# Softmax weights of a masked attention copied by transfers into a rounded-format tile and transposed from it two iterations later

## The chip, the cores and the metric

One core of one Trainium2 chip runs the whole program. The time is device microseconds from the profiler's clock; the kernel before is timed in three runs, and one further execution is profiled. TensorE is called PE, its weight loads PEld, VectorE DVE, ScalarE ACT, GpSimd POOL, and SyncE, which here only queues transfers, SP.

## What is computed

Attention over 4 batches of 8 heads, 576 tokens and 64 columns a head, in which scores that lie more than `tau` below their row's maximum are left out; then a mixture of 8 experts of which each token takes one; then a dense layer with a sigmoid-gated nonlinearity. The change touches the attention.

```python
def _attn_ref(q, k, v, tau):
    scale = 1.0 / np.sqrt(q.shape[-1])
    scores = scale * np.matmul(q, k.transpose(0, 1, 3, 2))
    thresh = np.max(scores, axis=-1, keepdims=True) - tau
    scores = np.where(scores >= thresh, scores, -1000000000.0)
    scores = scores - np.max(scores, axis=-1, keepdims=True)
    attn = np.exp(scores)
    attn = attn / (np.sum(attn, axis=-1, keepdims=True) + 1e-09)
    return np.matmul(attn, v)

def _moe_ref(x, modality_id, w_gate, modality_bias, w1, w2):
    logits = x @ w_gate + modality_bias[modality_id]
    e_idx = np.argmax(logits, axis=1)
    ...
    for e in range(E):
        mask = e_idx == e
        out[mask] = gate_w[mask, None] * (np.maximum(x[mask] @ w1[e], 0.0) @ w2[e])

def _moe2_ref(x, w_in, w_out):
    h = x @ w_in
    return (h * (1.0 / (1.0 + np.exp(-1.702 * h)))) @ w_out
```

## The kernel before

**Units.** Two heads make a pair; there are 16 pairs, and nine units to a pair (`UPP`), 144 in all. Units 0 to 7 are 128 queries of one head against its 576 keys; unit 8 holds the last 64 queries of both heads. A loop in `run` takes two units an iteration, 72 iterations, and one more to empty it. The order in which each engine works is the order in which the code issues.

**One iteration.** `qk` makes the scores of two units in PSUM (tile `sc`, L227), with queries and keys each split into a rounded part and a rest (`qkh`, `qkl`, type fp32r), so three products. `max` (DVE, L255) writes the shifted scores `e` and their extreme `thr`; `exp` (ACT, L261) exponentiates; `mask` (DVE, L285) drops what is below the threshold and writes the weights `E` (or `ET` for unit 8) and their row sum. The next unit on the same PSUM banks has to wait for that mask. `trans` (L313) transposes the weights of the two units of the iteration before, four 128x128 blocks a unit, in f32, into a PSUM tile `tr`, of which there are three; ACT copies it to `AT` (L315, L317). In four of nine iterations `trans_tails` (L331, L332, L335) transposes the last key columns, copied to `ATt` (L340). The table `AV` says how many value steps an iteration takes: four steps of products with V (L357), then a closing step (L363) and the copy to `xT` (L364), for each half of a pair. `ROW` says how many row items: products of `xT` with an identity and the gate's weights (L397), copied to `xr` (L402), scaled on POOL (L405, L410), and stored to `x_dram` by SP (L416).

**Loads.** SP queues a pair's queries and keys as one transfer of 896 KB (`F`, three buffers, L124) and its values (`V`, four buffers, L128) when a pair two or three earlier starts. POOL splits them, one piece an iteration: keys (L149 to L151), then queries of both heads. `sides` hands out small steps of the router (the choice of experts) between. `AVL`, `ROWL` and `SD` are the tables for the last batch's iterations, and `FILL` the number of dummy transposes that keep PE busy in the first ones. Behind the loop come the experts (L1033, L1077) and the dense layer (L1033, L1058), matmuls of fp32r parts with up to 512 columns.

## Time and profile before

| | us |
|---|---|
| median of 3 runs | 922.79 |
| lowest, highest | 922.45, 923.26 |
| the profiled execution | 921.75 |
| its span, first to last instruction | 920.0 |
| attention: first scores, last transposes | 5.7, 293 |

All durations below come from that one profiled execution. A busy time is the union of an engine's instructions, and matmuls overlap: an instruction's duration is longer than its distance to the next, so the length of a row of several shows more than the mean of one. The chain of waits goes back from the last instruction, at each step to what released it, and names the engine that held the end at that time. The table of windows gives each engine's busy time in a stretch, and at its end the granted clock, the mean share of the 16 DMA engines and their GB/s.

### The profile page before, as it was taken

What the parts mean: (1) busy time and instruction counts of PE and PEld (TensorE: products, weight loads), DVE (VectorE), ACT (ScalarE), POOL (GpSimd) and SP (SyncE); (2) the same over time, 40 slices, a digit from 0 to 9 for tenths busy, and PEclk for the clock granted to TensorE, in tenths of its full rate; (3) what the DMA queues carried; (4) which work ended last, traced back from release to release, by engine and by line L of the source; (5) the groups of instructions that cost most, each with busy time, mean ns of one, the idle gap of its engine ahead of it and who ended that gap; (6) DMA issues with size and microseconds to landing.
All of it is one profiled execution on the core that took longest, in us unless ns stands there. A gap on an engine that the chain in (4) does not pass through costs nothing.

```text
span 920.0 us, 14322 instructions
## 1 busy us (share of the span) xinstructions
PE 898.1 (98%) x5341; PEld 716.4 (78%) x5341; DVE 510.3 (55%) x1104; ACT 445.2 (48%) x787; POOL 233.2 (25%) x333
## 2 busy tenths in 40 slices
PE   9999999999999999999999999999999999999994
PEld 7677776776766788878889888888888888888894
DVE  7888889889787574678787588611111121111110
ACT  6777777777776533555545455422222222222221
POOL 7845655556544501010610000010001000100100
PEclk9999999999999999999999999999999999999997
DMA  7213432242102735465756153310001000100100
GB/s 257 73 46 122 140 128 72 71 131 74 36 9 76 239 103 187 142 230 178 229 183 231 68 184 117 112 46 12 24 12 46 7 12 7 46 0 1 46 1 26
DMA packets 53756, 85.67 MB, mean 93 GB/s; under 512 B 9300, under 2 KB 35058, under 8 KB 53682
## 3 DMA queue, kind: packets, MB, share of 16 engines
q1 hardware_dynamic: 50098, 74.63, 25.0%
q0 software_dynamic: 3312, 9.94, 3.3%
q8 instruction: 44, 0.72, 0.3%
q14 instruction: 30, 0.25, 0.1%
q10 hardware_dynamic: 272, 0.13, 0.0%
HBM read 67.57 MB, written 17.11 MB: 92 GB/s over the span
## 4 chain that ended last, share of the span: by engine, by line
PE 81%; DVE 7%; issue 6%; ACT 2%; DMA 2%; POOL 1%; SPq 0%; POOLq 0%; ACTq 0%
PE tr L1033 29%; PE sc L1058 19%; PE sc L1077 9%; PE sc L227 7%; PE av L357 6%; PE tr L313 6%; DVE E L285 3%; PE tr L397 2%; PE av L363 2%; DVE e L255 2%; ACT e L261 1%; DMA cv_raw<-in_moe_w_in_dram 1%; DMA xg<-y_first 1%; DVE bl L1303 1%; PE av L1005 1%
## 5 line engine op out<-in xcount | busy, mean ns | idle before, releaser
L1270 DVE TENSOR_TENSOR hl<-sg,hh 128x512 fp32r<-128x512 f32 (+1 forms) x80 | 51.1, 638 | 261.5 <-ACT hh L1268 259.1
L1267 ACT ACTIVATE sg<-tr 128x512 f32<-128x512 f32 (+1 forms) x80 | 44.3, 554 | 226.9 <-PE tr L1033 226.9
L261 ACT ACTIVATE e<-e,thr 128x576 f32<-128x576 f32 x144 | 109.6, 776 | 75.2 <-DVE e L255 74.6
L255 DVE TENSOR_SCALAR_CACHE_REDUCE e<-sc,taue 128x576 f32<-128x576 f32 x144 | 112.8, 815 | 33.7 <-PE sc L227 33.3
L1058 PE MATMUL sc<-wo_h,hh 128*128 128x512 f32 x288 | 112.2, 390 | 0.0
L1058 PE MATMUL sc<-wo_l,hh 128*128 128x512 f32 x288 | 112.2, 390 | 0.0
L1058 PE MATMUL sc<-wo_h,hl 128*128 128x512 f32 x288 | 112.0, 389 | 0.0
L285 DVE SCALAR_TENSOR_TENSOR E<-sc,thr,e 128x576 f32<-128x576 f32 x128 | 100.4, 813 | 5.1 <-ACT e L261 4.4
L1033 PE MATMUL tr<-xl,wi_h 128*128 128x512 f32 (+1 forms) x320 | 78.7, 368 | 0.0
L1033 PE MATMUL tr<-xh,wi_l 128*128 128x512 f32 (+1 forms) x320 | 78.7, 368 | 0.0
L1033 PE MATMUL tr<-xh,wi_h 128*128 128x512 f32 (+1 forms) x320 | 78.6, 368 | 0.0
L357 PE MATMUL av<-AT,V 128*64 128x288 f32 x512 | 77.3, 420 | 1.1 <-DVE ixs L933 0.6
L313 PE MATMUL tr<-ident,E 128*128 128x128 f32 x512 | 71.2, 279 | 0.0
L315 ACT COPY AT<-tr 128x512 f32<-128x512 f32 x128 | 68.2, 577 | 0.0
L1033 PEld LDWEIGHTS tr<-xh,wi_h 128*128 128x128 f32 x320 | 57.7, 188 | 11.1
L1033 PEld LDWEIGHTS tr<-xh,wi_l 128*128 128x128 f32 x320 | 56.9, 189 | 10.0
L1033 PEld LDWEIGHTS tr<-xl,wi_h 128*128 128x128 f32 x320 | 56.9, 189 | 9.9
L151 POOL TENSOR_TENSOR qkl<-F,qkh 128x640 fp32r<-128x640 f32 (+1 forms) x30 | 63.1, 2102 | 2.5
L313 PEld LDWEIGHTS tr<-ident,E 128*128 128x128 f32 x512 | 55.1, 141 | 10.3 <-issue 8.7
L1058 PEld LDWEIGHTS sc<-wo_h,hl 128*128 128x128 f32 x288 | 54.1, 188 | 11.3
L227 PE MATMUL sc<-qkh 64*128 64x288 f32 x320 | 57.0, 353 | 6.0 <-DVE E L285 4.2
L1058 PEld LDWEIGHTS sc<-wo_h,hh 128*128 128x128 f32 x288 | 54.1, 188 | 10.7
(262 smaller groups left out, 1578.2 us busy)
## 6 DMA issues: line engine op xcount, KB each, us to landing
F<-in_kq_dram SPq DMA_DIRECT2D x15, 896.0 KB
ra<-in_moe_w_dram SPq DMA_DIRECT2D x20, 512.0 KB
rb<-in_moe_w_dram SPq DMA_DIRECT2D x20, 512.0 KB
cv_raw<-in_moe_w_in_dram SPq DMA_DIRECT2D x16, 512.0 KB
cv_raw<-in_moe_w_out_dram SPq DMA_DIRECT2D x16, 512.0 KB
V<-in_vp_dram SPq DMA_DIRECT2D x16, 320.0 KB
x_dram<-xrow SPq DMA_DIRECT2D x72, 64.0 KB
y_rest<-blank SPq DMA_DIRECT2D x8, 256.0 KB
```

The costliest lines, as they stand in the source:

```text
L151: nc.gpsimd.tensor_sub(lo, x, hi.bitcast(F32))
L227: m = nc.tensor.matmul(self.banks[:, bank, 0:288], a[rs, q:q + 128], b[rs, k:k + 288], start=(n == 0), stop=(n == len(ops) - 1),).ins
L255: self.read(u, nc.vector.tensor_scalar(e, d["sc", w], self.taue[:, 0:1], 3.0e38, op0=ALU.add, op1=ALU.min, accum_out=thr))
L261: self.nc.scalar.activation(d["e", w], d["e", w], ACTF.Exp, bias=d["thr", w][:, 0:1], scale=-1.0)
L285: self.read(u, nc.vector.scalar_tensor_tensor(out=E.rearrange("p (a c) -> p a c", a=2), in0=d["sc", w], scalar=d["thr", w][:, 0:1], in1=d[ ...
L313: nc.tensor.transpose(tp[:, kc * 128:(kc + 1) * 128], E[:, k0 + kc * 128:k0 + (kc + 1) * 128], self.ident)
L315: return lambda: nc.scalar.copy(AT[:, h, :, c * 128:(c + 1) * 128], tp.rearrange("p (k c) -> p k c", k=4))
L357: nc.tensor.matmul(d["av"][h * 64:(h + 1) * 64, 0:288], d["V"][:, h, kc, :], d["AT"][:, h, kc, cols], start=(kc == 0), stop=False, skip_gr ...
L1033: nc.tensor.matmul(hps[:, 0:T], w[:, kd, :], blk[x][:, kd, 0:T], start=(i == 0), stop=(i == 11))
L1058: nc.tensor.matmul(y, h[:, cs], w, start=(f == 0 and i == 0), stop=(f == blk["nf"] - 1 and i == 2))
L1077: nc.tensor.matmul(blk["y"][d], w[:, ds], h[:, 0:T], start=(f == 0 and i == 0), stop=(f == last and i == 2))
L1270: return [upper, lambda: nc.vector.tensor_sub(hl, sg, hh.bitcast(F32))]
```

## The change

The weights are no longer transposed from `E`. Each unit's first 512 weights (for the second head of a pair, the last 512) go, behind its mask, by an SP transfer of 256 KB into a tile `R` of type fp32r (`lay`); the transfer copies the bits as they are. There are six such tiles. The transposes read `R` and an identity of the same type, two iterations after the scores instead of one, and stand at the end of the iteration, behind values and rows, with their copies at the end of ACT's. Tails are transposed as before. The tables of values and rows are new, and the last batch's have one iteration more. `F` has two buffers instead of three; a pair's load is two halves, each issued from POOL's list of pieces after the split that frees the buffer, and the queries are split one head at a time. Row stores are kept in a list and issued behind the next masks. The router's one sum of phase A uses a `tr` tile, the first iterations' dummy transposes are 60 instead of 54.

```diff
--- before.py
+++ after.py
@@ -25,12 +25,12 @@
 UPP = 9
 PJ = 9
 QW, KW = 1280, 640
-AV = (2, 2, 3, 3, 2, 2, 3, 2, 1)
+AV = (1, 3, 2, 3, 2, 2, 3, 2, 2)
 TURNS = ((0, 1), (2, 3))
 TAILS = {2: -1, 5: -2, 7: -2, 0: -1}
 IT_LAST = (NPAIR - HP) * UPP // 2
-AVL = (2, 2, 3, 2, 3, 2, 3, 2, 1, 2, 2, 3, 3, 2, 2, 3, 3, 2, 5)
-ROWL = (0, 1, 0, 1, 1, 1, 1, 1, 1, 0, 0, 0, 0, 1, 0, 1, 0, 1, 0)
+AVL = (1, 3, 2, 3, 2, 2, 3, 2, 2, 1, 3, 2, 3, 2, 2, 3, 2, 2, 1, 5)
+ROWL = (2, 0, 1, 0, 0, 1, 1, 1, 1, 1, 0, 0, 0, 0, 0, 0, 1, 0, 1, 1)
 NS0 = 7
 CA = (0, 1, 2, 2, 2, 2, 2, 2, 2, 2, 2, 2, 2, 2, 2, 2)
 CB = (0, 0, 0, 1, 0, 1, 0, 1, 0, 1, 0, 1, 0, 0, 0, 0)
@@ -40,12 +40,12 @@
 NBW = 6
 F0 = (0, 1, 0)
 NROW = 2
-FILL = (14, 12, 12, 12, 4)
+FILL = (14, 16, 12, 12, 6)
 SN = 1
 SD = (1, 2, 2, 2, 1)
 TAU_MAX = 104.0
 W_TOP = (1.875 - 2.0 ** -23) * 2.0 ** -96
-ROW = (0, 1, 0, 1, 1, 0, 1, 0, 1)
+ROW = (2, 0, 1, 0, 0, 0, 0, 1, 1)
 
 class Attention:
 
@@ -74,7 +74,8 @@
         self.banks = P("a_sc", 1, space=PSUM).tile([128, 4, 512], F32, name="sc")
         Q = lambda name, bufs: late_ctx.enter_context(tc.tile_pool(name=name, bufs=bufs, side="right"))
         cst = P("a_const", 1)
-        self.fp = P("a_f", 3)
+        self.fp = P("a_f", 2)
+        self.er = P("a_er", 6)
         self.ep = P("a_e", 4)
         self.ex = P("a_exp", 3)
         self.et = P("a_et", 2)
@@ -89,6 +90,8 @@
         self.rp = Q("a_rows", 2)
         self.rw = Q("a_xrow", 6)
 
+        self.idr = cst.tile([128, 128], F32R, name="idr")
+        nc.gpsimd.tensor_copy(self.idr, ident)
         self.cq = cst.tile([128, 1], F32, name="cq")
         self.taue = cst.tile([128, 1], F32, name="taue")
         self.tau = tau
@@ -118,10 +121,13 @@
                 )
 
 
-    def load(self, p):
-        d = self.st[p] = {}
-        d["F"] = F = self.fp.tile([128, KW + 2 * S], F32, name="F")
-        self.nc.sync.dma_start(F, self.kq[p])
+    def load(self, p, parts=(0, 1)):
+        if 0 in parts:
+            self.st[p] = {"F": self.fp.tile([128, KW + 2 * S], F32, name="F")}
+        n = (KW + 2 * S) // 2
+        for i in parts:
+            cs = slice(i * n, (i + 1) * n)
+            self.nc.sync.dma_start(self.st[p]["F"][:, cs], self.kq[p][:, cs])
 
     def load_v(self, p):
         V = self.vp.tile([128, 640], F32, name="V")
@@ -142,7 +148,9 @@
     def split(self, p, i):
 
         nc = self.nc
-        x, (hi, lo) = (self.keys, self.queries)[i](p)
+        x, (hi, lo) = self.queries(p) if i else self.keys(p)
+        if i:
+            x, hi, lo = (t[:, i - 1] for t in (x, hi, lo))
         if i == 0 and p == 1:
             nc.scalar.activation(x, x, ACTF.Copy, scale=self.cq[:, 0:1])
         elif i == 0:
@@ -296,6 +304,16 @@
             ]
 
 
+    def lay(self, u):
+
+        p, w = divmod(u, UPP)
+        d = self.st[p]
+        c, h = divmod(w, 2)
+        E = d["E", 4] if w == 8 else d["E", c][:, h]
+        k0 = 64 if w < 8 and h == 1 else 0
+        d["R", w] = self.er.tile([128, 512], F32R, name="R")
+        self.nc.sync.dma_start(d["R", w].bitcast(F32), E[:, k0:k0 + 512])
+
     def trans(self, u):
 
         nc = self.nc
@@ -304,13 +322,12 @@
         c, h = divmod(w, 2)
         if w == 0:
             d["AT"] = self.at.tile([128, 2, 4, S], F32, name="AT")
-            d["ATt"] = self.at.tile([128, S], F32, name="ATt")
-        AT, ATt = d["AT"], d["ATt"]
+        AT = d["AT"]
         tp = self.ps_tr.tile([128, 512], F32, name="tr")
-        E = d["E", 4] if w == 8 else d["E", c][:, h]
-        k0 = 64 if w < 8 and h == 1 else 0
+        R = d.pop(("R", w))
         for kc in range(4):
-            nc.tensor.transpose(tp[:, kc * 128:(kc + 1) * 128], E[:, k0 + kc * 128:k0 + (kc + 1) * 128], self.ident)
+            cs = slice(kc * 128, (kc + 1) * 128)
+            nc.tensor.transpose(tp[:, cs].bitcast(F32R), R[:, cs], self.idr)
         if w < 8:
             return lambda: nc.scalar.copy(
                 AT[:, h, :, c * 128:(c + 1) * 128], tp.rearrange("p (k c) -> p k c", k=4))
@@ -323,6 +340,8 @@
         nc = self.nc
         p, w = divmod(u, UPP)
         d = self.st[p]
+        if w == 3:
+            d["ATt"] = self.at.tile([128, S], F32, name="ATt")
         ATt = d["ATt"]
         c0 = 0 if w == 3 else 2
         n = 256
@@ -413,7 +432,8 @@
                 rr.unsqueeze(3).broadcast_to([w, 2, 2, 64]),
             )
             for u in range(2 if kc < 4 else 1):
-                nc.sync.dma_start(xd[b, 2 * kc + u][:, hh * 256:(hh + 1) * 256], xrow[u * 64:(u + 1) * 64, :])
+                self.stores.append(lambda u=u: nc.sync.dma_start(
+                    xd[b, 2 * kc + u][:, hh * 256:(hh + 1) * 256], xrow[u * 64:(u + 1) * 64, :]))
             if hh == 1 and kc == 4:
                 items, gate = self.router.gate_items(b, lgt)
                 self.side.extend([None] * (1 if b == B - 2 else NROW) + items + self.router.after_batch(b, gate))
@@ -428,27 +448,29 @@
         rest = self.first()
         self.load_v(0)
         self.load_v(1)
-        self.load(2)
-        self.poolq = []
+        self.poolq, self.stores = [], []
         self.avq, self.rowq, self.side = avq, rowq, side = [], [], []
         side += [None] * NS0 + [self.gate_setup, *self.router.setup_items(self.setup), *self.extra]
         it = done = 0
         while done < NU:
             last = it >= IT_LAST
             us = [u for u in (2 * it, 2 * it + 1) if u < NU]
-            ts = [u for u in (2 * it - 2, 2 * it - 1) if 0 <= u < NU]
+            ts = [u for u in (2 * it - 4, 2 * it - 3) if 0 <= u < NU]
             starts = [u // UPP for u in us if u % UPP == 0]
             for p in starts:
-                if p + 3 < NPAIR:
-                    self.load(p + 3)
-                if p + 2 < NPAIR:
+                if 0 < p < NPAIR - 2:
                     self.load_v(p + 2)
                 for n in range(1 if p == 0 else p + 2, min(p + 3, NPAIR)):
                     self.poolq += [lambda n=n, i=i: self.split(n, i) for i in range(2)]
+                    if n + 2 < NPAIR:
+                        self.poolq += [lambda n=n: (self.split(n, 2), self.load(n + 2, (0,)))]
+                        self.poolq += [lambda n=n: self.load(n + 2, (1,))]
+                    else:
+                        self.poolq += [lambda n=n: self.split(n, 2)]
             k = it % 9
             for u in us:
                 self.qk(u)
-            copies = [self.trans(u) for u in ts]
+            copies = []
             if it > 1 and k in TAILS:
                 copies.append(self.trans_tails(2 * it + TAILS[k]))
             for i in range(2):
@@ -461,12 +483,17 @@
                 c()
             while rest:
                 rest.pop(0)()
+            if it == 0:
+                self.load(2)
+                self.load_v(2)
             if self.norm:
                 self.norm.pop(0)()
             for i, u in enumerate(us):
                 self.mask(u)
+                self.lay(u)
                 if last:
                     self.sides(SD[i + 2], False)
+            self.store()
             if it < len(FILL) and FILL[it]:
                 warm = self.ps_av.tile([128, 512], F32, name="av")
                 for _ in range(FILL[it]):
@@ -477,6 +504,8 @@
             while m and rowq:
                 rowq.pop(0)()
                 m -= 1
+            for c in [self.trans(u) for u in ts]:
+                c()
             n = 1 if it else 2
             while n and self.poolq:
                 self.poolq.pop(0)()
@@ -489,12 +518,18 @@
                     avq += self.av_items(p, w // 8)
             it += 1
 
+    def store(self):
+
+        while self.stores:
+            self.stores.pop(0)()
+
     def tail(self, n):
 
         for _ in range(n):
             for q in (self.avq, self.rowq):
                 if q:
                     q.pop(0)()
+                    self.store()
                     break
         return bool(self.avq or self.rowq)
 
@@ -918,7 +953,7 @@
 
         def sum_up(c0, c1):
             if c0 == 0:
-                t["ip"] = self.ps_av.tile([128, 512], F32, name="av") if first else self.ps_tr.tile([128, 512], F32, name="tr")
+                t["ip"] = self.ps_tr.tile([128, 512], F32, name="tr")
             for c in range(c0, c1):
                 nc.tensor.matmul(
                     t["ip"][:, 0:2 * nh], OL[:, c, :], R[:, c].rearrange("p i h -> p (i h)"),
```

PE, the third iteration of nine. Before, between its scores and the next, with `L313` the main transposes, `L335` the tails, `L357` and `L363` value steps:

```order
L227 MATMUL sc<-qkh_139,qkl_140 128x288 x2
L313 MATMUL tr<-ident,E 128x128 x8
L335 MATMUL tr<-ident,E 128x128 x2
L357 MATMUL av<-AT,V 64x288 x4
L363 MATMUL av<-ATt,V 128x288
L227 MATMUL sc<-qkh_139 128x288 x2
```

Now, with `L330` the main transposes, `L354` the tails, `L376` and `L382` value steps:

```order
L235 MATMUL sc<-qkh_144,qkl_145 128x288 x2
L354 MATMUL tr<-ident,E 128x128 x2
L376 MATMUL av<-AT,V 64x288 x2
L382 MATMUL av<-ATt,V 128x288
L330 MATMUL tr<-idr,R 128x128 x8
L235 MATMUL sc<-qkh_144 128x288 x2
```

The eight transposes moved from ahead of the values to just ahead of the next scores, and read `R`; this iteration takes one value step fewer.

SP in the loop, before (`L416` row stores, `L1164` the router's blank rows):

```order
L1164 DMA y_rest<-blank 128x512
L124 DMA F<-in_kq_dram 128x1792
L128 DMA V<-in_vp_dram 128x640
L1164 DMA y_rest<-blank 128x512
L416 DMA x_dram<-xrow 64x256 x2
L1164 DMA y_rest<-blank 128x512 x2
```

Now (`L315` the copies to `R`, `L130` halves of `F`, `L134` values, `L435` row stores, `L1199` blank rows):

```order
L315 DMA R<-E 128x512 x2
L435 DMA x_dram<-xrow 64x256
L130 DMA F<-in_kq_dram 128x896
L1199 DMA y_rest<-blank 128x512
L134 DMA V<-in_vp_dram 128x640
L315 DMA R<-ET 128x512
L315 DMA R<-E 128x512
L130 DMA F<-in_kq_dram 128x896
```

Two copies an iteration now stand in the same queue as the loads and stores, and behind them.

ACT in the first iteration of nine, before:

```order
L261 ACTIVATE e<-e,thr 128x576 x2
L315 COPY AT<-tr 128x4x128
L317 COPY AT<-tr 128x4x2x64
L340 COPY ATt<-tr 128x320
L364 COPY xT<-av 128x288
```

Now, with the exponentials at `L269`, tails `L359`, `xT` at `L383`, rows `L421`, transposed weights `L332`:

```order
L269 ACTIVATE e<-e,thr 128x576 x2
L359 COPY ATt<-tr 128x320
L383 COPY xT<-av 128x288
L421 COPY xr<-tr 128x288 x2
L332 COPY AT<-tr 128x4x128 x2
```

The copies of transposed weights moved behind all others, and two row copies came into this iteration.

## Rows read from the trace of the kernel before

**Rows 1.** The page: busy time of PE, and its slices and clock.

```profile
PE 898.1 (98%) x5341; PEld 716.4 (78%) x5341; DVE 510.3 (55%) x1104; ACT 445.2 (48%) x787; POOL 233.2 (25%) x333
...
PE   9999999999999999999999999999999999999994
...
PEclk9999999999999999999999999999999999999997
```

**Rows 2.** Windows: us busy, PE, PEld, DVE, ACT, POOL; clock, DMA share, GB/s.

```profile
100.00:150.00 50.00, 48.49 (x406) 34.34 (x404) 42.67 (x110) 36.48 (x69) 27.27 (x30) 1.00 0.27 85
```

**Rows 3.** Chain of waits: start us, us, engine, tile and line; PE alone.

```profile
113.19 0.98 PE sc L227 x10
114.18 1.03 PE tr L313 x8
...
117.01 1.00 PE sc L227 x11
```

**Rows 4.** Chain of waits where it goes round the loop.

```profile
129.37 0.61 PE sc L227 x6
...
130.00 0.04 DVE e L255
...
130.92 0.79 ACT e L261
...
131.73 1.56 DVE E L285 x4
```

**Rows 5.** Waits of 20 to 280 us: who for whom, total, times, longest.

```profile
DVE e L255 <- PE sc L227: 31.9, 53, 1.2
PEld sc L227 <- DVE E L285: 17.5, 39, 1.6
...
PE sc L227 <- DVE E L285: 3.4, 6, 1.1
```

**Rows 6.** Line L313: ns min/median/max, first and last start.

```profile
L313 PEld LDWEIGHTS tr<-ident,E x512: 137/140/144, 10.8 to 292.7; 128*128 128x128 f32 x171
L313 PE MATMUL tr<-ident,E x512: 272/273/332, 10.8 to 292.8; 128*128 128x128 f32 x171
```

**Rows 7.** Groups by line and shape: count, busy us, mean ns, idle before.

```profile
L332 PEld LDWEIGHTS tr<-ident,ET 128*64 128x64 f32 x16 | 1.8, 111 | 0.0
L357 PEld LDWEIGHTS av<-AT,V 128*64 128x64 f32 x512 | 30.7, 136 | 24.4 <-issue 11.1 <-ACT xT L364 0.9 <-PE av L923 0.6
L1033 PEld LDWEIGHTS tr<-xh,ah 128*128 128x128 f32 x160 | 27.2, 188 | 5.0 <-ACT xh L1006 0.8 <-DVE xl L1007 0.2
L1033 PE MATMUL tr<-xh,al 128*128 128x512 f32 x128 | 34.4, 390 | 0.0
L1033 PE MATMUL tr<-xh,al 128*128 128x264 f32 x32 | 5.1, 282 | 0.0
L402 ACT COPY xr<-tr 128x288 f32<-128x288 f32 x32 | 13.0, 409 | 1.1 <-PE tr L397 0.2
```

**Rows 8.** Timeline: start us, length, instruction; the first load and its use.

```profile
0.74 0.42 ACTq L162 DMA_DIRECT2D F<-in_kq_dram  x1
...
2.94 0.40 ACT L192 CAST qkh<-F 128x256 fp32r<-128x256 f32 x1 [0.25 <-DMA F<-in_kq_dram]
```

**Rows 9.** Timeline: the loop's end, and runs of four rounded matmuls.

```profile
291.55 0.82 DVE L285 SCALAR_TENSOR_TENSOR ET<-sc,thr,e 128x576 f32<-128x576 f32 x1
...
292.88 0.60 PE L313 MATMUL tr<-ident,ET 128*128 128x128 f32 x4
...
485.22 0.64 PE L1033 MATMUL tr<-xh,ah 128*128 128x264 f32 x4
...
601.60 1.07 PE L1033 MATMUL tr<-xh,wi_h 128*128 128x512 f32 x4
```

**Rows 10.** The page, DMA queues: packets, MB, share of 16 engines.

```profile
q1 hardware_dynamic: 50098, 74.63, 25.0%
```

**Rows 11.** Waits of SP's queue, 20 to 290 us.

```profile
SPq L692 <- POOL lgt L388: 22.5, 1, 22.5
```

## The prediction

> **What bounds the kernel now.** The page comes first: TensorE (PE) is busy 98% of the span and its granted clock stands at 0.9 or more of full speed in all slices but the last [rows 1]. That says which engine to look at, not what it waits for. The change touches the attention loop alone, so the next view is busy time by stages of 50 us: in the loop PE is busy almost throughout, VectorE (DVE) 42.67 of 50 us, ScalarE (ACT) 36.48, GpSimd (POOL) 27.27, and the DMA engines 0.27 of the time [rows 2]. Two units make an iteration; the transposes run from 10.8 to 292.8 us, 71.5 iterations, so one takes 3.94 us [rows 6].
>
> The chain of waits shows who holds an iteration. Most are PE alone: scores 0.98, transposes 1.03, then values and rows, 3.82 us from 113.19 to 117.01, with no other engine in the chain [rows 3]. Others are the loop: scores at 129.37, maximum, exponential, and the second mask ends at 133.29 [rows 4]. This loop starts its first maximum at 130.00, so DVE can't start another sooner than 3.29 us later. The waits agree: in 260 us PE waits 17.5 + 3.4 us for masks, and DVE 31.9 us for scores [rows 5]. With 66 iterations in there PE waits 0.32 us in each, so its own work is about 3.62 us. DVE's is 42.67/50 of 3.94, 3.36 us. So PE binds, with DVE and the loop 0.3 us below it: that is how much room a faster PE has before another stream binds.
>
> **The transposes.** The change leaves the number of main transposes: 144 units of four, 576. What they cost now: one lasts 273 ns, but four in a row last 0.60 us, so they follow each other at (0.60 - 0.27)/3 = 0.109 us [rows 6, 9]. No transpose of the rounded type, and no matmul of it below 256 columns, is in this trace, so the new price is bounded from neighbours. Rounded matmuls of 512 and 264 columns last 390 and 282 ns, 0.4355 ns a column; at 128 columns that makes 282 - 136 x 0.4355 = 223 ns, 50 less than now [rows 6, 7]. Their spacing at 512 columns is (1.07 - 0.39)/3 = 0.227 us [rows 9], which less 384 x 0.4355 ns is 0.060 us. That is the value I take: 0.049 saved each, **28.2 us** in 576. The lower end is 0.4355 x 128 = 0.056 us, 30.5 us saved.
>
> The upper end hangs on the weight load before each transpose. For a matmul 128 columns of weights take 188 ns and 64 take 136: 0.8 ns a column, some 104 ns of real work behind a fixed 84. For a transpose 128 take 140 and 64 take 111: 0.45 ns a column, 58 ns of work [rows 6, 7]. I take the second slope, since the type doesn't seem to set it: f32 weights of a matmul (136 for 64 columns) and rounded ones (188 for 128) lie on one line, and only the transposes lie below. If a rounded transpose loses this, its spacing is 0.104 or more and nothing is won.
>
> The Trainium skill (TensorE: Matmul & The Clock Gate, section LDWEIGHTS) gives one price for all, columns divided by 1.2, 107 ns for 128, with no case for a transpose. By that the present 0.109 would be the weight load's, and the 576 transposes would save 1 us. The trace agrees for matmuls (0.8 ns a column), and disagrees for transposes (0.45).
>
> **The copies.** Each unit's weights E now go by a transfer of 256 KB from SBUF to SBUF into R, queued on SyncE (SP) behind the mask; the transpose follows two iterations later. The hardware queue moved 74.63 MB in 25.0% of 16 engines' 920 us, a rate of 324 GB/s while busy, so a copy needs 0.81 us of all engines and two 1.62 an iteration; with today's 0.27 x 3.94 = 1.06 that is 2.7 of some 3.6 us [rows 2, 10]. They fit. Latency: the first 128 KB of queries are issued at 0.74 and used at 2.94, 2.2 us [rows 8]; twice the size makes it 2.6; behind a 448 KB half of a load 4.0, behind V also 5.0. The cover: the second mask ends 3.92 us after its iteration starts [rows 4], and the transposes that need its copy close the iteration two later, so before the next scores there are 3 periods. At 3.55 us that leaves 10.65 - 3.92 - 0.6 = 6.1 us. So I cost landing at nothing; the cover ends at 6.1 us.
>
> SP works in order, and what waits there now holds the copies too. F halves wait for the last split of their pair's buffer, V loads for the values that free theirs, stores of rows and gates for POOL; a gate's store waited 22.5 us once [rows 11], with nothing urgent behind it. The change moves the row stores behind the next masks, where POOL is done, and the order has the freeing value step in the iteration of the V load, ahead of its masks. POOL's query split in two pieces costs one more pair of instructions a pair of heads on an engine that is 55% busy [rows 2]; it is hidden, unless POOL is late for an F half.
>
> **What the new order gives back.** ACT copies the transposed weights after everything else of its iteration, and PSUM has three "tr" tiles. In the iteration with two row items (once in nine), tails, two rows and two transposes ask for five tiles. The second transpose needs the first row's copy, which stands behind both exponentials (the second ends near 129.37 + 3.1), the tail copy, the xT copy and its own, about 0.41 each [rows 4, 7]: 3.1 + 1.25 = 4.35 us after the start. PE comes there after scores of 0.98 [rows 3] and, an estimate, 2.5 us of tails, values, rows and a transpose, at 3.45. That is 0.9 us lost, eight times: 7.2. In the others PE's work is near 3.2 us against DVE's 3.36, and I add 0.8. Together **8 us** back; ends: 0 if those waits fall into time PE now waits anyway, 14 if the loop takes half.
>
> **Start and end.** F has two buffers instead of three, so the third pair's load comes after the first scores; it is needed nine iterations later. Six more warm-up transposes, 0.65 us, lie in the first iterations, before the values start: nothing. At the end, before, the last mask starts at 291.55 and its transposes run at 292.88 [rows 9]. Now 2.6 us of landing and one more, nearly empty, iteration (tail, one value item, one row, two transposes, some 1.5 to 2 us) stand between: **1.5 us** lost, from 0.5 to 3.
>
> **The sum.** The profiled execution took 921.75 us, 1.75 around its span of 920.0. 921.75 - 28.2 + 8 + 1.5 = 903.05; the median of the runs lies 1.04 above it: **904 us**. PE's slices behind the loop all read 9 up to the last [rows 1], so what is won before 293 us arrives at the end whole.
>
> **Rivals.** (1) DVE and the loop take over: PE has 3.23 us of work, DVE 3.36, and an in-order pair so evenly loaded loses more than I take. At 14 us back: 910. For it: the even load; against: DVE waits 31.9 us for scores now, and these come earlier. (2) The rounded transpose is no faster, held by its weight load: at a matmul's 0.104 it saves 3 us, at 0.119 (the spacing of a 264-column rounded matmul, from its four in 0.64 us [rows 7, 9]) it loses 6; with half of the order's 8 and the end's 1.5 the time is 925 to 934. For it: no such transpose is in the trace; against: the two slopes. The rule of the Trainium skill (TensorE: Matmul & The Clock Gate, section LDWEIGHTS) would end here. If the type needed more passes it would be later still; no row bounds that. (3) On the other side, landing: three periods hold mask, landing and transposes, so a period is (3.92 + landing + 0.7)/3 at least. It equals today's 3.94 at 7.2 us of landing; each us beyond costs 72/3 = 24. At 8 us the time is 943. For it: SP's waits of many us ahead of copies [rows 11]; against: 2.6 to 5 us by the sizes. The place to see it is PE's wait for R.
>
> **How the numbers follow.** Forecast 904: 0.58. Loop takes over, 910 to 918: 0.18. No faster transposes: 0.14, of which a little still ends faster through the evened-out value tables. Late landing: 0.10, mostly slower. A measurement tells 0.2%, 1.8 us, from no change, so faster (under 921) 0.78, same 0.08, slower 0.14. The range takes in the forecast's bounds (30.5 saved, nothing back, 0.5 at the end: 893) and the first rival, to 921; the rest, 0.2, lies above.
>
> **What would show it.** Transposes on R of some 223 ns, spaced 0.06 us, with weight loads near 140; iterations of 3.6 us; the last transposes near 274 us; DVE's idle before maxima smaller, and no PE idle put down to R. It is wrong if R's weight loads last 188 or their spacing stays at 0.11, or if PE waits for transfers.

## The result, and the profile after

The changed kernel takes 929.31 us (median, 928.85 to 933.91) against 922.62 for the kernel before on the same chip (922.41 to 923.26): a ratio of 1.0085 over the runs (1.0073 by the medians), with an interval of 1.0073 to 1.0097. It is slower by 6.7 us, where 904 was forecast. Its profiled execution took 929.47 us, with a span of 927.2.

The page of the changed kernel, to hold against [rows 1, 10]: PE, VectorE, the slices of PE, its clock and of the DMA engines, and the hardware queue.

```profile
PE 891.4 (96%) x5347; PEld 711.3 (77%) x5347; DVE 508.7 (55%) x1104; ACT 449.2 (48%) x787; POOL 238.8 (26%) x364
...
PE   8999999999998999999999999999999999999994
...
PEclk9999999999998999999999999999999999999997
DMA  8577876765534735365746344310001000100100
...
q1 hardware_dynamic: 72994, 112.39, 36.6%
```

PE has less to do (891.4 us against 898.1) and fills less of its span: there is now one slice around the end of the loop in which both its share and its clock fall below nine tenths. The copies add 37.8 MB.

Line L330, the transposes of R (ns min/median/max, first and last start), and below it what ended PE's idle time before them (us in all, times). It answers to [rows 6].

```profile
L330 PEld LDWEIGHTS tr<-idr,R x576: 137/140/230, 16.5 to 300.2; 128*128 128x128 f32 x192
L330 PE MATMUL tr<-idr,R x576: 224/249/722, 16.6 to 300.2; 128*128 128x128 f32 x192
...
  issue: 11.1, 20
  DMA R<-E: 7.2, 9
  ACT ATt L359: 6.7, 17
  ACT e L269: 4.9, 9
```

The weight loads last 140 ns as forecast, and the shortest transpose 224, but the median one 249. The last transposes start at 300.2 us, not at the forecast 274. New is idle time ahead of them: for R itself, and for a `tr` tile that an ACT copy behind the exponentials has to free (before, these last waits came to 0.8 us).

How far a row of transposes has sped up is read from a row of eight: PE in the timeline (start, length), before in the first line, changed kernel in the second fence.

```profile
138.25 1.09 PE L313 MATMUL tr<-ident,E 128*128 128x128 f32 x8
```

```profile
115.72 0.87 PE L330 MATMUL tr<-idr,R 128*128 128x128 f32 x8
```

Seven distances in 1.09 - 0.27 us are 0.117 each, in 0.87 - 0.25 us 0.089. These rows include the step from one `tr` tile to the next. Between neighbours in one tile the commonest distance fell from 0.109 to 0.085 (the median to 0.086), so a transpose gained some 0.024 us, not 0.049.

Windows of the changed kernel (us busy, PE, PEld, DVE, ACT, POOL; clock, DMA share, GB/s), to hold against [rows 2], and its last iterations:

```profile
100.00:150.00 50.00, 48.25 (x427) 35.06 (x427) 41.80 (x112) 38.26 (x72) 26.03 (x37) 1.00 0.78 266
...
282.00:294.00 12.00, 8.88 (x72) 6.22 (x71) 8.38 (x25) 4.96 (x9) 4.06 (x7) 0.72 0.36 124
```

In this window the DMA share rose from 0.27 to 0.78, and between 282 and 294 us PE works 8.88 of 12 us at a mean clock of 0.72. What happened there is in two views: SP's queue with the issues and the time they took, and PE in the timeline (in brackets the idle time and what ended it).

```profile
283.55 1.29 SPq L727 DMA_DIRECT2D x_dram<-g  x2
284.95 8.08 SPq L315 DMA_DIRECT2D R<-E  x6
```

```profile
283.76 0.55 PE L330 MATMUL tr<-idr,R 128*128 128x128 f32 x4
287.44 0.72 PE L330 MATMUL tr<-idr,R 128*128 128x128 f32 x4 [3.12 <-DMA R<-E]
288.09 0.61 PE L235 MATMUL sc<-qkh 64*128 64x288 f32 x2
288.49 0.44 PE L235 MATMUL sc<-qkl,qkh 64*128 64x288 f32 x2
```

The gate's store waits on SP for the router's work on POOL; the copies behind it start at 284.95, PE idles 3.12 us, and from then on the scores last 0.61 and 0.44 us instead of 0.40 and 0.29: the granted clock is at its lower level, 1.2 GHz, for 6.8 us. In the loop it was there once before, for 3.4 us from 262.5, after an idle of 0.90 us for a mask.

Three points of the program show the balance, read from the first scores of an iteration (counted from 1) and the first product of the experts. Iteration 64 starts at 254.9 us before and 252.2 after; the experts start at 306.7 and 310.9; from there to the last matmul it takes 601.3 and 604.3. So the loop gained 2.7 us, its end lost 6.9, and the stage behind it 3.0.

### The profile page after: what moved, and what is told of

It reads as the page before. It is cut to its first block, busy times and chain, and to the rows that moved or that the text cites. A ratio compares the mean times of both kernels' runs of the same rounds, so it can differ in the third digit from the quotient of the medians.

```text
span 927.2 us, 14873 instructions
## 1 busy us (share of the span) xinstructions
PE 891.4 (96%) x5347; PEld 711.3 (77%) x5347; DVE 508.7 (55%) x1104; ACT 449.2 (48%) x787; POOL 238.8 (26%) x364
## 4 chain that ended last, share of the span: by engine, by line
PE 73%; issue 9%; DVE 5%; POOL 4%; DMA 4%; ACT 3%; SPq 0%; POOLq 0%; ACTq 0%; DVEq 0%
PE tr L1068 28%; PE sc L1093 19%; PE sc L1112 8%; PE sc L235 5%; PE av L376 5%; PE tr L330 3%; DMA R<-E 2%; DVE E L293 2%; PE tr L416 1%; DVE e L263 1%; PE av L382 1%; ACT e L269 1%; POOL qkl L159 1%; DMA cv_raw<-in_moe_w_in_dram 1%; DVE bl L1338 1%
## 5 line engine op out<-in xcount | busy, mean ns | idle before, releaser
L269 ACT ACTIVATE e<-e,thr 128x576 f32<-128x576 f32 x144 | 109.7, 776 | 65.9 <-DVE e L263 64.3
L376 PE MATMUL av<-AT,V 128*64 128x288 f32 x512 | 77.8, 425 | 0.9 <-ACT AT L334 0.9
L330 PE MATMUL tr<-idr,R 128*128 128x128 f32 x576 | 68.9, 260 | 8.1 <-DMA R<-E 5.2
L330 PEld LDWEIGHTS tr<-idr,R 128*128 128x128 f32 x576 | 56.1, 141 | 26.4 <-issue 11.1
L332 ACT COPY AT<-tr 128x512 f32<-128x512 f32 x128 | 70.3, 595 | 6.5 <-PE tr L330 5.7
L159 POOL TENSOR_TENSOR qkl<-F,qkh 128x576 fp32r<-128x576 f32 (+1 forms) x45 | 65.9, 1466 | 3.7
```

The lines of the kernel that those rows point to most:

```text
L159: nc.gpsimd.tensor_sub(lo, x, hi.bitcast(F32))
L269: self.nc.scalar.activation(d["e", w], d["e", w], ACTF.Exp, bias=d["thr", w][:, 0:1], scale=-1.0)
L330: nc.tensor.transpose(tp[:, cs].bitcast(F32R), R[:, cs], self.idr)
L332: return lambda: nc.scalar.copy(AT[:, h, :, c * 128:(c + 1) * 128], tp.rearrange("p (k c) -> p k c", k=4))
L376: nc.tensor.matmul(d["av"][h * 64:(h + 1) * 64, 0:288], d["V"][:, h, kc, :], d["AT"][:, h, kc, cols], start=(kc == 0), stop=False, skip_gr ...
```

## The experiments

Fifteen runs, each against the kernel before on its chip (median 922.6 to 922.9). "Base" is the kernel with rounded weights and the query split by heads.

**The type alone, and the type undone.** In the changed kernel, R back to f32:

```diff
-        d["R", w] = self.er.tile([128, 512], F32R, name="R")
+        d["R", w] = self.er.tile([128, 512], F32, name="R")
-            nc.tensor.transpose(tp[:, cs].bitcast(F32R), R[:, cs], self.idr)
+            nc.tensor.transpose(tp[:, cs], R[:, cs], self.ident)
```

> The changed kernel with the type alone undone: R and the identity are plain f32, all else stays (copies, order, tables, stores). Theory A, the type is worth what its spacing shows (0.085 us a transpose now against 0.109 before, 0.024 x 576 = 14 us): spacing back to 0.109, and the time is 929.3 + 10 to 14 = 939 to 943 us. Theory B, VectorE and the loop hold the iteration anyway, so that the faster transposes were absorbed: under 933 us.

936.96 us, ratio 1.0149 (1.0132 to 1.0166). The type is worth 7.6 us in the changed kernel, between both theories: about half of its 13.8 us (0.024 in 576) arrives. Part of the rest may be the clock: in the loop and its end it stood at its lower level for 3.4 us in this run and for 10.2 us in the changed kernel, an estimated 3.4 us of work lost.

In the kernel before, the type without copies, for the tails too:

```diff
-                d["E", c] = self.ep.tile([128, 2, S], F32, name="E")
+                d["E", c] = self.ep.tile([128, 2, S], F32R, name="E")
...
-            nc.tensor.transpose(tp[:, kc * 128:(kc + 1) * 128], E[:, k0 + kc * 128:k0 + (kc + 1) * 128], self.ident)
+            nc.tensor.transpose(tp[:, kc * 128:(kc + 1) * 128].bitcast(F32R), E[:, k0 + kc * 128:k0 + (kc + 1) * 128], self.idr)
...
```

> The kernel before with the type alone: masks write their weights rounded to fp32r, and all transposes read them directly in that type; no copies, old order and tables. The weights lose their low bits, so the output differs by that rounding. If the transfers slow the transposes of the changed kernel (0.085 us) and the type by itself gives 0.060: up to 28 us less, 895 to 902 us. If the weight load sets 0.085 without any traffic: 14 us less at most, 908 to 912 us. If the loop absorbs it: 916 us or more, with PE waiting longer for masks than the 17.5 + 3.4 us of before.

917.5 us, 0.994 (0.9924 to 0.9957); the profiled execution, from which the rows below come, took 921.59, the longest of the four. There is no added traffic, and the spacing is the same. PE in its timeline, main transposes (L315) and tails (L333, L334, L337):

```profile
75.69 0.53 PE L315 MATMUL tr<-idr,E 128*128 128x128 f32 x4
76.06 0.51 PE L315 MATMUL tr<-idr,ET 128*128 128x128 f32 x4
76.40 0.25 PE L333 MATMUL tr<-idr,ET 128*128 128x128 f32 x1
76.49 0.22 PE L334 MATMUL tr<-idr,ET 128*64 128x128 f32 x1
76.55 0.33 PE L337 MATMUL tr<-idr,E 128*128 128x128 f32 x2
```

All stream 128 columns. L333 loads 128 columns of weights and its successor follows 0.09 us later; L334 loads 64 and is followed after 0.06 (in all 16 of its rows 0.058 to 0.068). The kernel before, in f32:

```profile
75.66 0.27 PE L331 MATMUL tr<-ident,ET 128*128 128x128 f32 x1
75.77 0.27 PE L332 MATMUL tr<-ident,ET 128*64 128x128 f32 x1
75.88 0.38 PE L335 MATMUL tr<-ident,E 128*128 128x128 f32 x2
```

Here both are followed after 0.11, whatever the weights. So at this size the weight load sets the distance of rounded transposes, not of f32 ones, and traffic has no part in it. The gain was 5.1 us, of some 16.1 (0.024 in 576 main transposes and 96 of tails), and where the rest went is in the same trace: POOL, VectorE and PE at 207 us in the timeline, and then the windows around it.

```profile
206.82 2.66 POOL L153 TENSOR_TENSOR qkl<-F,qkh 128x1152 fp32r<-128x1152 f32 x1
...
207.15 2.38 DVE L660 TENSOR_TENSOR L<-L,bias 128x40 f32<-128x40 f32 x1
...
212.06 0.40 PE L229 MATMUL sc<-qkh 64*128 64x288 f32 x2 [1.81 <-DVE E L287]
```

```profile
206.00:212.00 6.00, 4.24 (x36) 3.05 (x36) 5.84 (x12) 3.56 (x8) 4.17 (x4) 1.00 0.04 11
212.00:220.00 8.00, 7.87 (x49) 5.95 (x50) 4.82 (x14) 4.02 (x8) 1.06 (x4) 0.57 0.04 10
```

A VectorE addition of 40 columns, elsewhere 0.2 us, lasts until POOL's subtraction ends; the masks are late, PE idles 1.81 us, and then its mean clock is 0.57 for 8 us. The kernel before has the same delay (its timeline):

```profile
136.57 2.65 POOL L151 TENSOR_TENSOR qkl<-F,qkh 128x1152 fp32r<-128x1152 f32 x1
...
137.09 2.18 DVE L658 TENSOR_TENSOR L<-L,bias 128x40 f32<-128x40 f32 x1
...
141.80 0.40 PE L227 MATMUL sc<-qkh 64*128 64x288 f32 x2 [1.12 <-DVE E L285]
```

but PE, slower, is idle for 1.12 us there, and its clock stays at 1.00. The Trainium skill (SBUF — State Buffer, section Who interferes with whom) says that VectorE and GpSimd share a pair of ports, taken for a whole instruction, by a VectorE instruction with two inputs in SBUF too. These rows agree: the small one ends with the large one.

**POOL's pieces and VectorE's small instructions.** The query split by heads (the line of the change) on rounded weights, and alone on the kernel before:

```diff
-        x, (hi, lo) = (self.keys, self.queries)[i](p)
+        x, (hi, lo) = self.queries(p) if i else self.keys(p)
+        if i:
+            x, hi, lo = (t[:, i - 1] for t in (x, hi, lo))
...
```

> The kernel before with rounded weights, transposed directly from where the mask writes them, and with POOL's query split made one head at a time, as in the change; no copies, old order and tables. The weights lose their low bits. In the run with the whole query split, three small VectorE instructions lasted 1.6 to 2.4 us instead of 0.2, each until POOL's subtraction of 2.66 us ended; PE waited 1.65 to 1.8 us for the mask behind them, and its clock was granted at 0.5 for 3.4, 3.4 and 6.8 us after that. Theory A, that is where the gain of the faster transposes went: pieces half as long halve the waits, the clock stays at 1.0, and the time falls from 917.5 by the some 9 us by which those six iterations were longer than their likes: 908 to 911 us. Rival, VectorE and the loop bind in any case and the clock is a by-product: 914 to 918 us.

914.85 us, 0.992 (0.9904 to 0.9937). The clock stays at 1.00 through the loop, but the time fell by 2.7 us, not by 9. The time is the rival's, but its reason isn't shown: small instructions still lasted up to 1.4 us beside the shorter pieces, and the next run but one takes 4 us off there.

> The kernel before with only POOL's query split made one head at a time. In the trace of before two small VectorE instructions lasted 2.18 us instead of 0.19, until POOL's subtraction of 2.66 us ended. Pieces half as long take off at most 1.3 us each: 920 to 922.6 us, that is no change or nearly none, if PE has other work beside these waits, since its clock never fell there. If it is slower, POOL's extra instructions cost something that the prediction took as hidden.

924.51 us, 1.0019 (1.001 to 1.0029): where PE has more work, the extra pieces give nothing and cost a little. In this trace five of the eight additions for the row sums (L296) last 1.4 us, where none took over 0.4 before; whether that is the cost no run tells.

The three small instructions that prepare the row sums, moved to POOL:

```diff
-                lambda: nc.vector.tensor_copy(rs[0:64, 4, h0:h0 + 4:2], rsT[0:64, hp - 1:hp + 1]),
+                lambda: nc.gpsimd.tensor_copy(rs[0:64, 4, h0:h0 + 4:2], rsT[0:64, hp - 1:hp + 1]),
...
-                lambda: nc.vector.tensor_scalar_add(r[:, :, h0:h0 + 4], rs[:, :, h0:h0 + 4], 1e-9),
+                lambda: nc.gpsimd.tensor_scalar_add(r[:, :, h0:h0 + 4], rs[:, :, h0:h0 + 4], 1e-9),
```

> The same base (914.9 us), with the two small copies and the addition that prepare the row sums moved from VectorE to POOL. On VectorE six of these in that base lasted 0.5 to 1.4 us instead of 0.16, each until POOL's subtraction ended. Theory: they wait for POOL whenever one of its two-input operations runs, and the masks behind them are late; on POOL they wait for nobody but their own turn: VectorE's excess falls from 6.7 us by some 4, the time by 1 to 3 us, 912 to 914 us. Rival: no gain, since other short VectorE operations then meet the same subtraction, or POOL's splits come later.

910.85 us, **0.9875** (0.9858 to 0.9891), 4.0 below the base: more than the 1 to 3 us expected, and the fastest of all (its weights are rounded to fp32r, so its output differs from both kernels' by that rounding). The groups by line, base first, then this kernel (count, busy us, mean ns):

```profile
L298 DVE TENSOR_SCALAR r<-rs 128x20 f32<-128x20 f32 x8 | 3.9, 488 | 0.0
L296 DVE COPY rs<-rsT 64x2 f32<-64x2 f32 x8 | 3.0, 373 | 0.0
```

```profile
L298 POOL TENSOR_SCALAR r<-rs 128x20 f32<-128x20 f32 x8 | 2.2, 270 | 0.7
```

> The kernel before with only those small copies and the addition moved from VectorE to POOL: the control for the 910.9 us of the rounded base with the same move. In before they lasted some 2 us longer in all than undisturbed, and PE has more work to hide behind: 920 to 922.5 us if PE binds, as the prediction said. If it wins as much as there (4 us, 918.8), VectorE's delays were on the path before the change already, and the prediction's reading that PE alone binds was too simple.

923.07 us, 1.0003 (0.9993 to 1.0013): the control. The move gives nothing while PE is slower, so these waits were hidden before, and became the bound with the faster transposes.

> Rounded weights, the whole query split in one piece on POOL as before, and the small copies on POOL: the 917.5 us run with one fix, without the other. The router's two additions that lasted 2.4 us on VectorE meet POOL's subtraction of 2.66 us still. If it is those that the split by heads cures: low clock at some 141 and 213 us remains, not at 49, and the time lies between 910.9 and 917.5, at 913 to 915 us. If the norm copies were the larger part: 911 us.

916.26 us, 0.9925 (0.9908 to 0.9943), above the 913 to 915 expected. This cure without the split gives 1.2 of 6.7 us, which isn't clear of noise (the interval overlaps that of 917.5), and the split without this cure gave 2.7: the router's additions still last 2.4 us, and the clock still falls at 138 and 210 us. It takes both.

**Copies against direct reading.** The change's order without its copies:

```diff
-                self.lay(u)
...
-        R = d.pop(("R", w))
+        R = E[:, k0:k0 + 512]
...
```

> The changed kernel without the copies: the mask writes rounded weights, the transposes read them there, still two iterations later and at the end of the iteration (six weight tiles instead of four, which take the room of R). The weights lose their low bits. If traffic slows the transposes: spacing 0.06 and 929.3 - 14 - 7 (end) = 908 us. If only the waits for R and the end hang on the copies: spacing stays 0.085, 7.2 us of waits in the loop and about 7 us at the end go, of which the first may be absorbed: 915 to 922 us. If the copies cost nothing but the end: 922 us.

918.88 us, 0.9958 (0.9941 to 0.9974), at a spacing of 0.086: the second case. With the base this gives the bill: type and split by heads -8.0 us (922.9 to 914.85), the order, tables, halves of loads and the later end +4.0 (to 918.88), the copies +10.4 (to 929.31). The last isn't pure: base and this run round the tails as well, the changed kernel doesn't, and 96 transposes at 0.024 us make up to 2.3 of the 10.4.

The gate's stores on POOL's queue:

```diff
-                nc.sync.dma_start(dst, g16[u * 64:(u + 1) * 64, 0:n])
+                nc.gpsimd.dma_start(dst, g16[u * 64:(u + 1) * 64, 0:n])
```

> The changed kernel with the gate's two stores moved from SP to POOL's own queue, so that nothing that waits for the router stands ahead of the last copies. Theory A, the end was lost to that one store: the last R lands before PE wants it, the stall of 3.1 us and the low clock of 6.8 us behind it go (3.1 + 3.4), and the time is 929.3 - 6.5 = 923 us, with the last transposes near 293. Rival: the last iterations are late by themselves (landing of 3.1 us and an iteration with nothing else to do), PE idles there anyway and the clock falls anyway: 926 us or more.

926.4 us, 1.0036 (1.0026 to 1.0047): 2.9 of the 6.5 us, the rival's time. The stall and the low clock behind it are gone (the earlier one stays, 3.4 us from 263.1), but PE still idles 0.7 us each for a `tr` tile and a mask. Windows of this run:

```profile
282.00:294.00 12.00, 10.53 (x104) 7.89 (x103) 10.05 (x28) 8.18 (x17) 8.25 (x13) 1.00 0.45 144
```

Copies queued by ACT:

```diff
-                self.lay(u)
...
+            for u in us:
+                self.lay(u)
...
-        self.nc.sync.dma_start(d["R", w].bitcast(F32), E[:, k0:k0 + 512])
+        self.nc.scalar.dma_start(d["R", w].bitcast(F32), E[:, k0:k0 + 512])
```

> The changed kernel with the copies queued by ACT at the end of each iteration instead of by SP behind the masks: nothing of SP's (loads, row stores, the gate's store) stands ahead of a copy any more, and none waits behind one. Theory A, what the copies cost beyond direct reading (+1.3 us in the first iterations, +1.6 in the loop, +4 in the last iteration and the low clock behind it) is their place behind others in SP's queue: 929.3 - 6 = 923 us, with no PE wait for R. Rival, each issue occupies ACT and each copy starts later, after ACT's copies of transposed weights: the waits for R stay or grow, 930 us or more.

945.84 us, 1.0254 (1.0237 to 1.0272). The issues hold up ACT (0.51 us each in the mean, 144 times), its exponentials, and so the masks. PE's longest idle time, in its timeline, and VectorE's waits for exponentials, 20 to 280 us (total, times, longest):

```profile
33.23 0.61 PE L235 MATMUL sc<-qkh 64*128 64x288 f32 x2 [5.23 <-DVE E L293]
```

```profile
DVE E L293 <- ACT e L269: 19.9, 29, 5.9
```

In the changed kernel the waits came to 4.2 us. Theory A fell, the rival's time holds. Yet SP's transfers were in the way here too: before that idle ended, ACT's queue had stood 7.15 us ahead of a copy's issue, until the semaphore that this copy shares with a half of `F`, queued by SP at 26.86, was set at 30.25. Whether another queue could carry the copies for less isn't answered.

Copies that nobody reads, on the base, into two tiles of their own:

```diff
                 self.mask(u)
+                self.lay(u)
...
```

> The kernel with rounded weights and the query split by heads (914.9 us), plus the two copies an iteration into R, queued on SP behind the mask as in the change, but read by nobody. It tells what the transfers cost by being there. Theory A, only waiting for R costs: 914.9 to 916 us. Theory B, the traffic itself slows other transfers and engines: the start of the loop, and the experts' stage, which took 604.4 us from its first matmul to the last of the program in all five kernels with copies against 601.3 to 601.8 in the four without; then 918 us or more. The transposes' spacing should stay at 0.085 us in either case.

917.82 us, with runs from 916.23 to 921.57; 0.9942 (0.9925 to 0.996). It lies between the theories: 3.0 us at the median for the copies' presence. That isn't clear of noise, since its interval overlaps the base's (0.9904 to 0.9937); the two fastest runs are at 916.2 and 916.4, the base's at 914.0 and 914.6. The experts' stage isn't longer (601.9 us). In its profiled execution a mask waited once 1.3 us for a copy that still read its tile. What is left of the 10.4 us, the tails' share aside, would then hang on using R, which no run took apart.

Two fixes in the changed kernel, the gate's stores and the row sums on POOL:

> The changed kernel with two fixes: the gate's stores on POOL's queue (926.4 us alone) and the row sums' small copies and addition on POOL instead of VectorE (worth 4.0 us on the base with rounded weights). Theory A, VectorE's small instructions hold masks back here as well (3.8 us of excess in the loop, and the low clock at 262 us behind a late mask): 926.4 - 3 = 923 us, the time of the kernel before. Theory B, the changed order hides them, and only the copies and the end cost: 926 us again.

925.53 us, 1.0042 (1.0022 to 1.0062). Theory B: 0.9 us less than with the first fix alone is within noise, and mended as far as this, the changed kernel is still behind.

**The order.** The transposes ahead of the values, as they were:

```diff
-            copies = []
+            copies = [self.trans(u) for u in ts]
...
-            for c in [self.trans(u) for u in ts]:
-                c()
```

> The changed kernel with the transposes and their copies put back where they were in the iteration, right behind the scores and ahead of tails, values and rows; still two iterations later, still from R. Theory A, the place at the end costs: PE comes to the transposes when the tiles tr wait for ACT's copies behind the exponentials, and to the next scores when the mask isn't done, with nothing to do between; ahead of the values the tiles are free, and the waits of 4.5 (ATt) + 4.0 (exponential) + 2.3 + part of 11 us go: 929.3 - 8 = 921 us. Theory B, R lands just before it is used and would be late by the some 2 us that the transposes come earlier: PE's wait for R grows from 4.5 us to some 20 us and the time is 935 us or more.

954.89 us, 1.0336 (1.0317 to 1.0355): theory B by the time, though PE's waits for R come to 9.9 us, not 20, and the row items (L416) wait another 8.0 for ACT's copies. The clock was also at its lower level six times up to 530 us. Waits of PE, 20 to 280 us:

```profile
PE tr L416 <- ACT AT L332: 8.0, 13, 1.1
PE tr L330 <- DMA R<-E: 7.4, 12, 2.9
PE tr L330 <- DMA R<-ET: 2.5, 2, 1.3
```

With these copies, two iterations ahead, the transposes are better off at the end. Then, the row items spread:

```diff
-ROW = (2, 0, 1, 0, 0, 0, 0, 1, 1)
+ROW = (1, 1, 1, 0, 0, 0, 0, 1, 1)
-ROWL = (2, 0, 1, 0, 0, 1, 1, 1, 1, 1, 0, 0, 0, 0, 0, 0, 1, 0, 1, 1)
+ROWL = (1, 1, 1, 0, 0, 1, 1, 1, 1, 1, 0, 0, 0, 0, 0, 0, 1, 0, 1, 1)
```

> The changed kernel with the two row items of the first iteration of nine spread over two iterations (1, 1, 1 instead of 2, 0, 1), nothing else. Theory A, the prediction's term for what the order gives back: the second transpose waits for the first row's copy, 0.9 us eight times (the first iteration of nine lasts 4.57 us against 3.8 of its neighbours): 929.3 - 6 = 923 us. Rival, that iteration is long for its tails and its five tiles in any case, or the time reappears in the next one: within 2 us of 929.3.

929.72 us, 1.0073 (1.0046 to 1.0099). The rival: the first iteration of nine fell from 4.41 to 3.95 us in the mean, the second rose from 3.75 to 3.89, the third from 4.48 to 4.60, the fourth from 3.52 to 3.85.

One value step and one row item moved in the base:

```diff
-AV = (2, 2, 3, 3, 2, 2, 3, 2, 1)
+AV = (2, 2, 3, 3, 2, 2, 2, 3, 1)
-ROW = (0, 1, 0, 1, 1, 0, 1, 0, 1)
+ROW = (0, 1, 0, 1, 0, 1, 1, 0, 1)
```

> The same base (914.9 us), with one value step moved from the seventh to the eighth iteration of nine, and one row item from the fifth to the sixth. By the nine iterations' means of that base (4.38 and 4.09 us where PE has most to do, 3.49 in the sixth and the eighth) PE holds the long ones and VectorE with the loop the short ones. If so, evening them out gives some 0.3 to 0.5 us in each of seven periods: 911 to 913 us. If the long ones are long for another reason: 914 to 916 us.

932.49 us, 1.0098 (1.0081 to 1.0115): slower, which neither case expected. The long iteration got shorter (4.38 to 3.69), but the moved step meets a closing step in the next, whose result ACT has to copy out of the one `av` bank first: PE waited 12.2 us for `xT`, in six waits, and that iteration takes 5.89. The clock fell after three of these waits.

## Why the prediction was wrong

Term by term, the forecast of -28.2, +9.5 and 0 us became -8.0, +4.0 and +10.4: 20.2 - 5.5 + 10.4 us make 25.1 of the 25.3 between 904 and 929.3.

**The transposes (28.2 us).** The term was mis-sized by half: 0.024 us each, 13.8 us in 576. The step that failed is the spacing of 0.060, carried over from rows of 512 columns [rows 9], where the weight load is hidden. The slope of 0.45 ns a column wasn't the fault ((0.09 - 0.06)/64 is 0.47): what it left out is the fixed part, some 0.03 us, which each weight load adds as well. It was taken as free. That the type doesn't set the slope was read from two points, one of each type, and two points always lie on one line; it held all the same, R's loads last 140 ns. Of the Trainium skill's two figures the 107 ns cited is above the row; another (TensorE: Matmul & The Clock Gate, section Back-to-back issue gap, about 81 ns for a load and a matmul of 128 columns) lies near the measured 85.

**What binds.** "PE binds, with DVE and the loop 0.3 us below it" was right for the kernel before: taking work off VectorE there gives nothing (923.07). As a mean, the gain (0.024 x 8, 0.19 us an iteration) would have fitted into that room. What the mean hid are single iterations in which VectorE waits for POOL: the type alone gave 5.1 of some 16.1 us until these waits were taken off, and then, with the split by heads, 11.9. The prediction saw that split as one more pair of instructions on POOL, and not what it does to VectorE, though the 2.18 us row was in the trace of before.

**The copies (0 us).** They cost 10.4, less up to 2.3 for the tails. Latency was priced well (2.6 to 5 us forecast; measured from issue to landing, median):

```profile
R<-E SPq DMA_DIRECT2D x128, 256.0 KB, 3.1
```

and in mid-loop R is mostly there in time. What failed is "with nothing urgent behind it": at the end of the loop the last copies stand behind the gate's store, and that stall with its low clock is 2.9 us. The copies' presence on the base is 3.0 at the median, not clear of noise. No run splits the rest by cause, but the two profiled executions, with copies and without, show where it lies. Up to the start of iteration 6 it is 1.3 us (24.8 against 23.5; the first R came 0.72 us late). From there to iteration 64 it is 1.6, no more than the tails' type can explain (an estimated 1.9 in 58 iterations). To iteration 72 it is 4.0, where the stall and the earlier low clock lie, then 1.3 to the experts and 2.5 in their stage, below.

**The order (8 us) and the end (1.5 us).** Together they lost 4.0 us instead of 9.5. The mechanism named, the two row items, was there as waits for ACT's copies, but it wasn't the price: spread out, the time reappeared in the neighbours. The end was under-priced: from the start of iteration 72 to the experts it takes 18.0 us in the base and 21.5 in the changed order without copies, 3.5 more; the upper bound was 3. So the loop itself gave back little: iteration 72 starts 1.4 us later (281.2 against 279.8 in the profiled executions).

**"What is won before 293 us arrives at the end whole".** Not quite. In each of the seven kernels that are the changed one with its copies, PE idles 2.5 to 3.8 us in the experts' stage, in all others 0.4 to 1.8. PE's waits in the changed kernel between 375 and 410 us, and VectorE's (375 to 525) ahead of them:

```profile
PE av L1040 <- DVE xl L1042: 1.4, 1, 1.4
...
DVE cv_e L1238 <- DMA cv_raw<-in_moe_w_in_dram: 6.1, 4, 4.0
```

A load of weights lands later there (without copies the longest of these waits is 2.3), VectorE waits for it in order, and PE waits for what stands behind. Why it lands later 70 us after the last copy is open.

**Rivals.** The second, "no faster transposes", has the right time (925 to 934) for a wrong reason. The third, landing, was real mainly at one place (3.1 of 7.2 us of waits for R), and through what stood ahead in SP's queue, not through the size. The first, VectorE taking over, is what the type alone ran into, with a cause that the text hadn't named. None of the three priced several losses at once, and it was their sum that turned the sign.

## What to carry to other kernels

An operation that isn't in the trace is priced from a neighbour that is limited by the same thing: here a row in which each instruction loads as many weights as it streams columns, not one in which the stream hides the load. Before an engine that binds by a few per cent is made faster, list what the next one waits for, its smallest instructions too: hidden delays become the bound, and the clock fell behind some of them. And when latency-bound transfers join a queue, look at what stands ahead of them at each stage, the last iterations above all.

## What the runs showed of the hardware

- Rounded transposes of 128x128 follow each other at 0.085 to 0.09 us, f32 ones at 0.109; with 64 columns of weights, the rounded one's successor comes after 0.06, the f32 one's after 0.109.
- A small VectorE addition with two inputs lasted 2.18 to 2.4 us instead of 0.2, until POOL's subtraction of 2.66 us ended; copies of 64x2 up to 1.57 instead of 0.16.
- PE's granted clock went to its lower level after idles of 1.81 us (rounded weights, 212 us) and 3.12 us (changed kernel, 287 us), and stayed at 1.00 after one of 1.12 us in the kernel before. The length alone doesn't tell: it also fell after 0.90 us (changed kernel, 262 us), and with one value step moved it fell after three waits of 1.79 to 2.07 us (35, 73 and 148 us) and stayed after three of 2.07 and 2.08 (112, 187 and 224 us).
- 256 KB from SBUF to SBUF, queued by SP among other transfers, landed 3.1 us after issue (median of 128); with two an iteration the DMA share of the loop (20 to 270 us) was 0.67 instead of 0.27.
- Issued from ACT, the same transfers held up its exponentials: masks waited 19.9 us for these instead of 4.2.
